# Seven half-size products for the first chunk of an MLP's second layer, in a fused attention and Fourier-mix kernel

## The chip, the cores and the metric

The kernel runs on one NeuronCore of a Trainium2 chip. A core has a matrix engine (TensorE, PE in the profile; PEld is its loading of weights), a vector engine (VectorE, DVE), a scalar engine (ScalarE, ACT), GpSimd (POOL) and a sync engine (SyncE, SP), which issues most of the transfers between the chip's main memory and the core's memory, SBUF. TensorE writes to PSUM, eight banks of 2 KB for each of 128 partitions. Every engine works through its own instructions in order and waits for others by semaphores. The metric is the time of one execution on the device in microseconds; the median of three runs before is 1942.89 us.

## The reference

Eight batches, eight heads, 576 tokens, head size 64. Attention keeps the 32 largest scores of each row; the heads are put side by side (512 channels), and then comes a Fourier mix and an MLP, all in float32:

```python
scores = scale * np.matmul(q, k.transpose(0, 1, 3, 2))
kth = np.partition(scores, -top_k, axis=-1)[..., -top_k:-top_k + 1]
scores = np.where(scores >= kth, scores, -1000000000.0)
attn = softmax(scores)                    # written out in the original
x = np.matmul(attn, v)                    # -> (8, 576, 512)
mixed = np.real(np.fft.fft(np.fft.fft(x, axis=1), axis=2))
u = x + mixed
un = (u - mean(u)) / np.sqrt(var(u) + 1e-06)
ch = np.maximum(un @ w_ch1, 0.0) @ w_ch2  # 512 -> 2048 -> 512
out = u + ch
```

## The kernel before

The attention is cut into 288 items: for each batch four pairs of heads, and for each pair nine items of 128 rows (tokens by one head, the last 32 tokens of each half of the sequence gathered into a fifth "tail" tile of 64 rows). The main loop makes one step per item. In step `i` TensorE makes the scores of item `i + 3` (`scores`, L346), transposes the exponentials of item `i - 2` (`transposes`, L411) and now and then multiplies them by v (`attend`, L448). VectorE finds the 32 largest of each row in four rounds of eight (`top_ops`, L367 and L369). GpSimd makes the two numbers of each row that the mask needs (`bounds`, `nt`) and subtracts the mask (`mask`, L384), ScalarE does the rest of the mask (L383), the exponential (`expo`, L390) and the copies out of PSUM.

When a batch's attention is done, the Fourier mix follows as matmuls with tables (`fold_ops`, `dft_tokens` L607, `dft_channels` L656), then the mean and variance (`stats`), the transposes of the mixed tile (`channels_first`, L720) and the MLP. A batch's 576 tokens are two chunks: chunk 0 has tiles 0, 1 and the tail tile 4 (320 columns), chunk 1 has tiles 2 and 3 (256 columns). `mlp_units` cuts the MLP into units: for each chunk 16 of `hidden` (first layer and relu, L742 and L746; `hT` holds the 2048 hidden channels as 16 blocks of 128), and then for each tile its part of the second layer, `back`: 16 matmuls of 512 columns into one bank `cp` (L766), in eight units of two. The tail tile has four units of L802. A tile of chunk 0 is then scaled by the inverse deviation on ScalarE (L791) and added into `x` on GpSimd (L792); tile 3 is added by VectorE (L780). `store` sends the tile out two steps later.

The order is written out by hand. Each step has a list of fixed TensorE work, and between its entries `some` takes units from the queue of the MLP. How many is set by `level`: from the units' planned costs (1.75 for a unit of `back`, 8 * width / 1200 for one of `hidden`) and the planned cost of each step's fixed work it finds the level at which the queue is empty when the next batch's MLP arrives (`arrivals`). Batch b's MLP is therefore spread over steps of the attention of batches b + 1 and b + 2. Batch 7's comes after the last attention step, alone. On GpSimd a step's order is: the mask of the item before, the plan's early work (`pool0`), `bounds`, late work (`pool`, `pool2`). SyncE issues loads of q, k and v at fixed steps, four or five steps ahead of their use, and the stores of the plan's `load2`.

The weights `w2` lie in SBUF as `w2[:, it, :]`, 16 blocks of 128 hidden channels by 512 output channels. `ps_m` is a pool of three PSUM banks, from which `hp`, `cp`, the Fourier tiles and the transposed tiles take their banks.

Of the kernel before, what the change touches and what calls it, by code (L numbers as in the profile page):

```python
# [64 lines left out]
def kernel(  # L65
# [42 lines left out]
    small = ctx.enter_context(tc.tile_pool(name="small", bufs=4))  # L108
    ps_s = ctx.enter_context(tc.tile_pool(name="ps_s", bufs=2, space=bass.MemoryType.PSUM))
    ps_t = ctx.enter_context(tc.tile_pool(name="ps_t", bufs=2, space=bass.MemoryType.PSUM))  # L110
    ps_o = ctx.enter_context(tc.tile_pool(name="ps_o", bufs=1, space=bass.MemoryType.PSUM))
    ps_m = ctx.enter_context(tc.tile_pool(name="ps_m", bufs=3, space=bass.MemoryType.PSUM))

# [36 lines left out]
    def weight_steps(chunks, space, wc, slots):  # L150
# [16 lines left out]
        def scale_high(n):  # L167
            if moe_w_ch1.dtype == F32:
                return
            scaled[n] = ps_m.tile([P, wc], F32, name=f"wh_{n}", tag="mm")  # L170
            nc.scalar.activation(
                out=scaled[n], in_=words(n)[2], func=AF.Copy, scale=2.0 ** -112
            )
# [112 lines left out]
    def scores(i, part):  # L286
# [22 lines left out]
        if part == 1:  # L309

            pool, tag = (ps_s, "sp") if i else (ps_m, "mm")
            copy = nc.scalar.copy if i else nc.vector.tensor_copy
            sp = pool.tile([P, NF * P], F32, name=f"sp_{i}_t", tag=tag)
# [164 lines left out]
    def to_tokens(pair, ch, at_once=True):  # L478
# [6 lines left out]
        pool, tag = (ps_o, "o") if at_once else (ps_m, "mm")  # L485
        tp = pool.tile([P, 4, P], F32, name=f"tpx_{pair}_{ch}", tag=tag)
# [106 lines left out]
    def dft_tokens(b, par):  # L593

# [3 lines left out]
        if b not in y_of:  # L598
            y_of[b] = batp.tile([P, 4, S], F32, name=f"y_{b}", tag="y")
        y = y_of[b]  # L600
        yps = [
            ps_m.tile([P, 2, KQ], F32, name=f"yp_{b}_{par}_{g2}", tag="mm") for g2 in range(2)
        ]

        def mm(g2, gg, st, lhsT, rows, table, start=False):

            nc.tensor.matmul(  # L607
                yps[g2][0:rows, gg, :],
# [8 lines left out]
        for g2 in range(2):  # L617
            for gg in range(2):
                g = 2 * g2 + gg
                for st in range(3):  # L620
                    f = fg[:, st] if st < 2 else ftail
                    mm(g2, gg, st, f[:, P * g:P * (g + 1)], P, gg, start=gg == 0 and st == 0)
        for st in range(3):
            mm(0, 1, st, zw[:, st, Q1:Q1 + 1] if st < 2 else ftail[:, DM:DM + 1], 1, 0)
# [5 lines left out]
        for g2, yp in enumerate(yps):  # L630
            y2 = y[:, 2 * g2:2 * g2 + 2, :]
            nc.scalar.copy(out=y2[:, :, par:HS + 1:2], in_=yp[:, :, 0:KQ - par])
            nc.scalar.copy(out=y2[:, 0, mir], in_=yp[:, 0, back])
            nc.scalar.mul(out=y2[:, 1, mir], in_=yp[:, 1, back], mul=sg[:, g2:g2 + 1])
        if par == 1:
            tails_of_y(b)
        return 4.3
# [6 lines left out]
    def dft_channels(b, t, quick=False):  # L644

        rows, y = ROWS[t], y_of[b]
        mp = ps_m.tile([P, 2, DM // 2], F32, name=f"mp_{b}_{t}", tag="mm")
# [62 lines left out]
    def channels_first(b, t):  # L710
# [7 lines left out]
        tp = ps_m.tile([P, NDT, P], F32, name=f"tpu_{b}_{t}", tag="mm")  # L718
# [5 lines left out]
        return 0.6  # L724

    def mlp_units(b):
# [4 lines left out]
        def hidden(ch, it):  # L733
# [6 lines left out]
            hp = ps_m.tile([P, CW[0]], F32, name=f"hp_{b}_{ch}_{it}", tag="mm")  # L740
# [7 lines left out]
        cps, cts = {}, []  # L748

        def ct_of(t):  # L750


            if t == 2:
                return hTs[1].rearrange("p i c -> p (i c)")[:, NIT * CW[1]:NIT * CW[1] + DM]
            if not cts:
                cts.append(batp.tile([P, 3, DM], F32, name=f"ct_{b}", tag="fold_s"))
            return cts[0][:, CHUNKS[0].index(t), :]

        def back(ch, t, part):
            n, hT, rs = CHUNKS[ch].index(t), hT_of[ch], rs_of[b]  # L760
            if part == 0:
                cps[t] = ps_m.tile([P, DM], F32, name=f"cp_{b}_{t}", tag="mm")
            cp = cps[t]
            if t != 4:
# [5 lines left out]
                if part == 7:  # L770
                    xt = x[:, t, :]

                    def store():
                        tok = HS * (t // 2) + P * (t % 2)
                        nc.sync.dma_start(out=out[b, tok:tok + P, :], in_=xt)
                        if t == 3:
                            written.add(b)

                    def finish():
                        nc.vector.scalar_tensor_tensor(  # L780
                            out=xt, in0=cp, scalar=rs[:, t:t + 1], in1=xt, op0=ALU.mult, op1=ALU.add
                        )

# [5 lines left out]
                    else:  # L789
                        ct = ct_of(t)  # L790
                        nc.scalar.mul(out=ct, in_=cp, mul=rs[:, t:t + 1])  # L791
                        nc.gpsimd.tensor_tensor(out=xt, in0=xt, in1=ct, op=ALU.add)  # L792
# [15 lines left out]
            if part == 3:  # L808
                ct = ct_of(t)
                for h in range(2):  # L810
                    r0 = TAIL + TH * h
                    nc.scalar.copy(out=ct[TH * h:TH * (h + 1), :], in_=cp[r0:r0 + TH, :])

                def finish():
                    xt, c = x[0:TAIL, 4, :], ct[0:TAIL]
                    nc.vector.tensor_tensor(out=c, in0=cp[0:TAIL], in1=c, op=ALU.add)
                    nc.vector.scalar_tensor_tensor(
                        out=xt, in0=c, scalar=rs[0:TAIL, 4:5], in1=xt, op0=ALU.mult, op1=ALU.add
                    )
                    for h in range(2):  # L820
                        tok = HS * h + 2 * P
                        nc.sync.dma_start(
                            out=out[b, tok:tok + TH, :], in_=x[TH * h:TH * (h + 1), 4, :]
                        )

                if last:
                    finish()
                else:
                    late_next.append(finish)

        units = []
        for ch in range(2):
# [4 lines left out]
            for t in CHUNKS[ch]:  # L837
# [110 lines left out]

    for b in range(B):
# [42 lines left out]
        for n, t in enumerate((0, 1, 4, 2, 3)):  # L992
# [7 lines left out]
            if first and t == 4:  # L1000
                at(s + 1, "pe", lambda: (queue.extend(held), held.clear()) and 0.0)
        at(s + 1, "begin" if quick else "dve", lambda b=b: rsqrt(b))
        arrivals.append(s + (1 if quick else 2))
        at(arrivals[-1], "units", lambda b=b: (queue if b else held).extend(mlp_units(b)))

    queue, held, pending, written, now, out_next = [], [], [], set(), [0], []
# [14 lines left out]
    def level(i):  # L1021

        steps = range(i, next((a for a in arrivals if a > i), i + PER_BATCH))
        rest, lev = sum(u[0] for u in queue + held), 0.0
# [23 lines left out]
    while i < N + 4 or plan or queue:  # L1048
# [23 lines left out]
        if pending and pending[0][0] <= i:  # L1072
# [121 lines left out]
```

## Time and profile before

| | us |
|---|---|
| median of three runs (1942.6 to 1943.57) | 1942.89 |
| the profiled execution | 1944.57 |
| its span, first to last instruction | 1942.8 |
| TensorE busy | 1831.8 |
| VectorE busy | 1577.0 |
| ScalarE busy | 1205.3 |
| GpSimd busy | 773.3 |
| L766, tiles 0 to 3 of the second layer, busy | 477.2 |
| L742, first layer, busy | 539.0 |

The profile is of one execution. A group's row names the line, the engine, the operation, what is written and read, and the size; then come the count, the busy time, the mean duration in ns of one, the idle time of the engine before it and who ended it. A float32 matmul stands there as two records, one for each pass over the moving operand. Matmuls are pipelined: a pass lasts longer than the distance to the next one. The work of the MLP lies at these times (first layer of chunk 0, then tiles 0 and 1 of the second):

| batch | first layer, chunk 0 | tiles 0 and 1 |
|---|---|---|
| 1 | 513.6 to 567.2 | 567.4 to 611.7 |
| 2 | 745.5 to 798.7 | 799.7 to 838.9 |
| 4 | 1184.9 to 1237.7 | 1238.7 to 1282.0 |
| 6 | 1624.6 to 1676.9 | 1676.7 to 1714.0 |
| 7 | 1814.2 to 1848.8 | 1848.6 to 1876.2 |

The last attention step's mask is at 1734.4 us.

### The profile page before, as it was taken

The numbers are of one execution on the slowest core, as the hardware profiler recorded it, in microseconds if no ns is written. First come the engines' busy times: TensorE is split into PE (matmuls) and PEld (weight loads), VectorE is DVE, ScalarE is ACT, GpSimd is POOL, SyncE is SP. The second block draws the span as 40 slices with busy tenths as digits, with TensorE's granted clock in tenths as the row PEclk, the third lists the DMA queues.
The fourth block names the chain that finished last, engine by engine and source line by source line (L and its number), as shares of the span: only waits on it lengthen the run. The fifth ranks groups of instructions, "written<-read, shape, count | busy, mean of one in ns | idle before, by whom it ended". The sixth has DMA issues, their size and how long they took to land.

```text
span 1942.8 us, 27224 instructions
## 1 busy us (share of the span) xinstructions
PE 1831.8 (94%) x8624; PEld 1123.4 (58%) x8624; DVE 1577.0 (81%) x3245; ACT 1205.3 (62%) x3060; POOL 773.3 (40%) x1054
## 2 busy tenths in 40 slices
PE   6567799999999999999999999999999999998999
PEld 3344465564665656556664756556664756566655
DVE  8999989999999999888888879988888879843000
ACT  6878657776876667666666667666666757541100
POOL 4768642326523454235423444235523444222000
PEclk8877899999999999999999999999999999999999
DMA  5333000101001010010100110010000100000000
GB/s 164 105 90 106 19 13 19 33 19 30 19 19 33 19 30 13 13 33 19 30 19 19 27 24 21 11 33 19 24 19 24 27 24 19 1 14 1 11 14 11
DMA packets 133583, 57.80 MB, mean 30 GB/s; under 512 B 124352, under 2 KB 124480, under 8 KB 133440
## 3 DMA queue, kind: packets, MB, share of 16 engines
q1 hardware_dynamic: 132656, 55.85, 10.8%
q8 instruction: 69, 1.13, 0.2%
q14 instruction: 74, 0.61, 0.1%
q10 hardware_dynamic: 784, 0.21, 0.0%
HBM read 46.57 MB, written 9.44 MB: 29 GB/s over the span
## 4 chain that ended last, share of the span: by engine, by line
PE 79%; DVE 7%; POOL 7%; ACT 4%; issue 3%; DMA 0%; SPq 0%; POOLq 0%; DVEq 0%; ACTq 0%
PE hp L742 24%; PE cp L766 22%; PE o L448 7%; PE tpP L411 6%; PE sp L346 6%; PE yp L607 3%; DVE m L367 3%; PE cp L802 3%; DVE wk L369 2%; PE mp L656 2%; POOL wk L384 2%; PE sp_t L316 2%; POOL w L198 1%; POOL w L197 1%; PE tpk L260 1%
## 5 line engine op out<-in xcount | busy, mean ns | idle before, releaser
L384 POOL TENSOR_TENSOR wk<-S,wk 128x576 f32<-128x576 f32 x288 | 407.2, 1414 | 907.8 <-ACT wk L383 854.6
L367 DVE MAX8 m<-wk 128x8 f32<-128x576 f32 x864 | 623.7, 750 | 5.5
L742 PE MATMUL hp<-unT,w 128*128 128x256 f32 (+1 forms) x2048 | 539.0, 410 | 3.1 <-ACT unT L723 2.1
L766 PE MATMUL cp<-w,hT 128*128 128x512 f32 x1024 | 477.2, 598 | 0.0
L742 PEld LDWEIGHTS hp<-unT,w 128*128 128x128 f32 x2048 | 373.5, 191 | 126.2 <-issue 31.4
L369 DVE MATCH_REPLACE8 wk<-m,wk 128x576 f32<-128x576 f32 x576 | 427.7, 743 | 0.0
L766 PEld LDWEIGHTS cp<-w,hT 128*128 128x128 f32 x1024 | 179.4, 190 | 180.5 <-issue 179.9
L390 ACT ACTIVATE wk<-wk,nt 128x576 f32<-128x576 f32 x288 | 225.6, 783 | 54.3 <-POOL wk L384 53.4
L411 PE MATMUL tpP<-ident,wk 128*128 128x128 f32 x1152 | 185.4, 285 | 65.6 <-ACT wk L390 42.0
L414 ACT COPY PT<-tpP 128x512 f32<-128x512 f32 (+1 forms) x320 | 171.8, 549 | 119.1 <-PE tpP L411 116.5
L383 ACT ACTIVATE wk<-S,nt 128x576 f32<-128x576 f32 x288 | 227.7, 791 | 27.9 <-POOL nt L376 26.5
L411 PEld LDWEIGHTS tpP<-ident,wk 128*128 128x128 f32 x1152 | 140.9, 145 | 162.9 <-ACT wk L390 60.9
L746 ACT ACTIVATE hT<-hp 128x320 f32<-128x320 f32 (+1 forms) x256 | 105.1, 411 | 193.3 <-PE hp L742 191.0
L367 DVE MAX8 m<-S 128x8 f32<-128x576 f32 x288 | 214.0, 743 | 12.2 <-ACT S L320 11.9
L369 DVE MATCH_REPLACE8 wk<-m,S 128x576 f32<-128x576 f32 x288 | 213.8, 742 | 0.0
L448 PE MATMUL o<-PT,v 128*64 128x256 f32 (+3 forms) x1440 | 196.0, 416 | 2.1 <-ACT PT L414 1.6
L349 ACT COPY S<-sp 128x512 f32<-128x512 f32 (+1 forms) x264 | 142.2, 590 | 65.9 <-PE sp L346 65.6
L346 PE MATMUL sp<-kT,qT 64*128 64x512 f32 (+1 forms) x528 | 162.1, 675 | 4.3 <-ACT means L934 3.3
L448 PEld LDWEIGHTS o<-PT,v 128*64 128x64 f32 x1440 | 111.7, 153 | 75.7 <-issue 17.5
L780 DVE SCALAR_TENSOR_TENSOR x<-cp,gi,x 128x512 f32<-128x512 f32 x11 | 8.2, 746 | 128.3 <-PE cp L766 128.3
L316 PEld LDWEIGHTS sp_t<-kt,qT 128*128 128x128 f32 x320 | 56.4, 197 | 53.8 <-issue 20.0
L346 PEld LDWEIGHTS sp<-kT,qT 64*128 64x128 f32 (+1 forms) x528 | 43.0, 193 | 62.8 <-issue 44.5
(126 smaller groups left out, 1822.6 us busy)
## 6 DMA issues: line engine op xcount, KB each, us to landing
space<-in_moe_w_ch_dram SPq DMA_DIRECT2D x32, 512.0 KB, 3.6
nat<-in_q_dram SPq DMA_DIRECT2D x128, 64.0 KB, 2.1
v<-in_v_dram SPq DMA_DIRECT2D x128, 64.0 KB, 2.1
out_dram<-x SPq DMA_DIRECT2D x32, 256.0 KB, 2.1
nat<-in_k_dram SPq DMA_DIRECT2D x124, 64.0 KB, 2.1
nat<-in_q_dram SPq DMA_DIRECT2D x128, 8.0 KB, 1.7
v<-in_v_dram SPq DMA_DIRECT2D x128, 8.0 KB, 1.7
nat<-in_k_dram SPq DMA_DIRECT2D x124, 8.0 KB, 1.7
```

The source lines that it names most:

```text
L346: nc.tensor.matmul(sp[r], lhsT=qT[hd, q_cols], rhs=kT[hd, :], start=True, stop=True)
L349: nc.scalar.copy(out=s_t[r, keys], in_=sp[r])
L367: ops.append(lambda src=src, m8=m8: nc.vector.max(out=m8, in_=src))
L369: ops.append(lambda src=src, m8=m8: nc.vector.match_replace(w, m8, src, NEG))
L383: nc.scalar.activation(out=w, in_=Ssb[i], func=AF.Relu, scale=-FAR, bias=Nt[i][:, 1:2])
L384: nc.gpsimd.tensor_tensor(out=w, in0=Ssb.pop(i), in1=w, op=ALU.subtract)
L390: nc.scalar.activation(out=w, in_=w, func=AF.Exp, bias=Nt.pop(i)[:, 0:1], accum_out=den_t[pair % 3][:, c:c + 1],)
L411: nc.tensor.transpose(tp[:, c, :], p_sb[:, k0 + P * c:k0 + P * (c + 1)], ident)
L414: nc.scalar.copy(out=pt[:, NF * he:NF * (he + 1), col:col + w], in_=tp[:, :, o:o + w])
L448: nc.tensor.matmul(o[D * e:D * (e + 1), c0:c1], lhsT=vv[:, c, e, :], rhs=pt[:, 2 * NF if c == NF else NF * e + c, c0:c1], start=(c == 0), ...
L742: nc.tensor.matmul(hp[:, 0:w], lhsT=w1[:, dt, P * it:P * (it + 1)], rhs=unT[:, dt, 0:w], start=(dt == 0), stop=(dt == NDT - 1),)
L766: nc.tensor.matmul(cp, lhsT=hT[:, it, P * n:P * (n + 1)], rhs=w2[:, it, :], start=(it == 0), stop=(it == NIT - 1),)
```

## The change

For batches 1 to 7, tiles 0 and 1 of the second layer are no longer two rows of 16 matmuls. Write the two tiles' hidden values as four quarters (tile by half of the 2048 hidden channels: A11, A12, A21, A22) and w2 as four quarters (half of the hidden channels by half of the output channels: B11, B12, B21, B22). The four quarters of the result are put together from seven products of quarters, each of eight matmuls of 256 columns:

| unit | product | bank, half | place of w2's part |
|---|---|---|---|
| `p2` | A12 B21 | v, low | w2_21, as it is |
| `p1` | A11 B11 | w, low | w2 |
| `p5` | (A21 + A22) T1 | v, high | w2_12 |
| `p4` | A22 T4 | w, high | w2_21 (batch 7: a place of its own) |
| `p6` | (A21 + A22 - A11) T2, onto p1 | w, low | w2_12 |
| `p3` | (A12 - that) B22, onto p5 | v, high | w2 |
| `p7` | (A11 - A21) T3, onto w low | w, low | w2_21 (batch 7: a place of its own) |

T1 = B12 - B11, T2 = B22 - T1, T3 = B22 - B12, T4 = B21 - T2. They are made once on GpSimd during batch 1's attention (`parts_of_w2`, 16 steps of two subtractions) and kept in main memory (`scr`), with copies of B12 and B21. During the products `bring` fetches them in halves of 512 KB into the places of B12 and B21 within w2, each as soon as the product before has read the half, and in the end B12 and B21 again. The sums of the hidden quarters (`mix`) are made in place in `hT` on GpSimd, in halves; they wait in a list, `sums`, which each step works off within a planned time (`some_sums`), or sooner where a product needs one (`need`). Five results are scaled on ScalarE and added into `x` on GpSimd, two are added by VectorE; in batch 7 VectorE adds all seven. Each product is two units of planned cost 1.75.

The banks of `ps_m` are given out by `bank` in turn, past those that are held; the two banks of the products are held throughout. `dft_tokens` now makes its two halves one after the other, and in batch 7 the Fourier tiles and the transposed tiles take banks of other pools. `written` is set when four tiles are stored, and `to_tokens` isn't done in the steps of an `attend` from step 76 on.

```diff
+    def bank(shape, name, hold=False):
+        while turn[0] in held:
+            turn[0] = (turn[0] + 1) % 3
+        n = turn[0]
+        turn[0] = (n + 1) % 3
+        t = ps_m.tile(shape, F32, name=name, tag=f"m{n}", bufs=1)
+        if not hold:
+            return t
+        held.add(n)
+        return t, lambda: held.discard(n)
...
+    scr = dramp.tile([P, len(OPS), NK, DH], F32, name="w2_parts", tag="w2_parts")
+    w2_12, w2_21 = w2[:, 0:NK, DH:DM], w2[:, NK:NIT, 0:DH]
+
+    def bring(o, place, part):
+        kcs = slice(NK // 2 * part, NK // 2 * (part + 1))
+        dst = place[part] if isinstance(place, list) else place[:, kcs]
+        nc.sync.dma_start(out=dst, in_=scr[:, o, kcs, :])
...
+        for out_, in0, in1 in sums[2 * half:2 * half + 2]:
+            nc.gpsimd.tensor_tensor(out=t[:, out_], in0=in0, in1=in1, op=ALU.subtract)
+        if half:
+            at(now[0] + 1, "load2", lambda: nc.sync.dma_start(out=scr[:, 0:4, kc, :], in_=t))
...
+    def some_sums(limit):
+        while sums and sums[0][1] <= limit:
+            key, us, fn, _ = sums.pop(0)
+            limit -= us
+            fn()
+            summed.add(key)
...
+            def product(name, cols, a, rhs_of, part, start):
+                dst = half_bank(name, cols)
+                for kc in range(NK // 2 * part, NK // 2 * (part + 1)):
+                    nc.tensor.matmul(
+                        dst, lhsT=h()[a][:, kc, :], rhs=rhs_of(kc), start=start and kc == 0,
+                        stop=kc == NK - 1, skip_group_check=True,
+                    )
+                return dst
...
+            def p5(part):
+                need((b, "21", part))
+                c = product("v", hi, "21", first, part, False)
+                bring(T2, w2_12, part)
+                if part:
+                    to_x(tb, hi, c, 2)
+
+            def p4(part):
+                c = product("w", hi, "22", in_second, part, False)
+                bring(T3, second, part)
+                if part:
+                    to_x(tb, lo, c, 3)
+                    mix("22", "22", "11")
+
+            def p6(part):
+                need((b, "11", part))
+                c = product("w", lo, "11", first, part, False)
+                bring(B12, w2_12, part)
+                if part:
+                    to_x(ta, hi, c, 4)
...
+            def p7(part):
+                need((b, "22", part))
+                c = product("w", lo, "22", in_second, part, False)
+                if not last:
+                    bring(B21, second, part)
+                if part:
+                    to_x(tb, slice(0, DM), c, None, lambda: (banks["w"][1](), store(tb)))
...
-            for t in CHUNKS[ch]:
+            if b and ch == 0:
+                begin, products = fast()
+                units[1:1] = begin
+                units += products
+            for t in (4,) if b and ch == 0 else CHUNKS[ch]:
...
+        planned = 1.5 * len(plan.get((i, "pool0"), [])) + 1.3 * len(plan.get((i, "pool2"), []))
         run(i, "pool0")
+        some_sums(max(2.1 - planned, 0.0))
         bounds(i)
+
+        some_sums(1.3)
```

In the program as it is built, the order on each engine is fixed. The prediction speaks of it: which instructions of other work stand on TensorE between two products, and which waits stand before a product.

## The prediction

> **What bounds the kernel now.** I read the page first: busy shares, then the slices.
>
> ```profile
> PE 1831.8 (94%) x8624; PEld 1123.4 (58%) x8624; DVE 1577.0 (81%) x3245; ACT 1205.3 (62%) x3060; POOL 773.3 (40%) x1054
> ...
> PE   6567799999999999999999999999999999998999
> ...
> DVE  8999989999999999888888879988888879843000
> ```
>
> One slice is 48.6 us. TensorE is full from the seventh slice on; before that no MLP work exists and VectorE sets the pace. A busy TensorE need not be at its peak, so I looked at the stages in which the changed products lie (batch 1 at 567 us, batch 2 at 800 us, batch 4 at 1239 us; columns: PE, PEld, DVE, ACT, POOL).
>
> ```profile
> core 0: us, PE busy (x) PEld busy (x) DVE busy (x) ACT busy (x) POOL busy (x), PEclk, DMA share, GB/s
> 567.00:612.00 45.00, 45.00 (x194) 22.68 (x192) 43.74 (x91) 29.03 (x76) 15.11 (x18) 1.00 0.11 26
> 800.00:852.00 52.00, 52.00 (x212) 23.62 (x209) 44.39 (x91) 30.09 (x77) 15.64 (x19) 1.00 0.07 18
> 1238.70:1282.00 43.30, 43.30 (x175) 20.76 (x168) 38.06 (x77) 27.38 (x69) 12.13 (x15) 1.00 0.08 21
> ```
>
> In batch 1's stage VectorE is busy for 43.74 of 45.00 us, so two engines are full. From batch 2 on VectorE has 5 to 8 us to spare, and the waits of 800 to 1640 us say for whom it waits:
>
> ```profile
> DVE wk L369 <- PE tpP_t L422: 43.9, 16, 5.0
> ```
>
> It waits for TensorE's transposes. So in batches 2 to 6 a microsecond off TensorE is a microsecond off the span, and in batch 7's MLP, where nothing else runs, all the more. The pace of one matmul pass is read there, in TensorE's timeline (start, length, count):
>
> ```profile
> 1876.40 7.09 PE L802 MATMUL cp<-w,hT 128*64 128x512 f32 x32
> 1883.42 27.89 PE L742 MATMUL hp<-unT,w 128*128 128x256 f32 x128
> 1911.15 27.63 PE L766 MATMUL cp<-w,hT 128*128 128x512 f32 x64
> ```
>
> The last pass shows its own duration, the others the distance to the next. With the groups' 0.59 us for 512 columns: (27.63 - 0.59)/63 = 0.429 us. With 0.38 us for 256 columns: (27.89 - 0.38)/127 = 0.217 us. An f32 matmul is two passes.
>
> **The products.** Removed in each of batches 1 to 7: two tiles of 16 matmuls of 512 columns, 64 passes x 0.429 = 27.5 us. Added: seven products of 8 matmuls of 256 columns, 112 passes x 0.217 = 24.3 us. TensorE gains 3.2 us a batch, 22.4 us in all.
>
> A rule speaks against this. The Trainium skill ("TensorE: Matmul & The Clock Gate", Part 3, The mechanism) lists that a weight load overlaps running matmuls only when their row groups differ. Here all use the whole array, and there are 112 loads where there were 64. With the 0.190 us that a load takes in the trace, the old batch would cost 64 x 0.619 = 39.6 us, the new one 112 x 0.407 = 45.6 us: 42 us slower over seven batches. But L742 loads new weights for each of its 128 passes of 256 columns and still starts one every 0.217 us. I take the row.
>
> **Work on other engines**, from the groups split by shape:
>
> ```profile
> L492 DVE TENSOR_TENSOR x<-tpx,rd 128x256 f32<-128x256 f32 x57 | 24.1, 423 | 55.4 <-PE tpx L488 54.0
> L414 ACT COPY PT<-tpP 128x256 f32<-128x256 f32 x64 | 21.1, 389 | 9.8 <-PE tpP L411 9.6
> L930 POOL TENSOR_TENSOR w<-w,means 128x512 f32<-128x512 f32 x16 | 20.1, 1274 | 0.0
> L792 POOL TENSOR_TENSOR x<-x,ct 128x512 f32<-128x512 f32 x14 | 17.8, 1275 | 11.3 <-ACT ct L791 9.3 <-DVE wk L369 1.9
> L549 POOL TENSOR_TENSOR zt<-x 64x256 f32<-64x256 f32 x16 | 11.3, 724 | 0.0
> L791 ACT ACTIVATE ct<-cp,gi 128x512 f32<-128x512 f32 x14 | 9.6, 688 | 8.0 <-PE cp L766 7.5
> L780 DVE SCALAR_TENSOR_TENSOR x<-cp,gi,x 128x512 f32<-128x512 f32 x11 | 8.2, 746 | 128.3 <-PE cp L766 128.3
> ```
>
> GpSimd, a batch: eight sums of hT quarters at 1.27 us and five adds into x at 0.72, less two adds at 1.275 = +11.2 us. Its cover is its own idle time, 60% of the span and some 4 us of each 6 us step. What is queued behind a sum is the next nt and mask, whose exponential TensorE transposes a step later; uncovered it would cost all 11.2 us. In the built order the sums of hT come at least 9 us of TensorE work before the product that needs them (7 in batch 7). The table of w2's sums is 32 subtractions x 0.72 = 23 us once, 1.4 us in each of 16 steps where GpSimd is under half busy: nothing. ScalarE: five scalings of 0.39 for two of 0.69, +0.6 us. VectorE: 0.42 + 0.75 = +1.2 us, from the two last adds. In batches 2 to 6 its 5 to 8 us of slack hide that. In batch 1 the slack is 1.26 us against 1.2 added, so I book no gain there. In batch 7 the adds are all VectorE's, which is idle there.
>
> **Two new waits of TensorE.** First, products six and four share a bank: four writes its high half, six then accumulates in its low half. By addresses alone six needn't wait for the reader of four. The Trainium skill ("PSUM — Partial Sum Buffer", PSUM bank collisions raise a hardware error) says that two engines must be kept apart by bank even at disjoint columns; no run here shows that error, but the built order holds the wait: six starts only after the scaling of four's result. The price: the end of the last pass, 0.38 - 0.22, a reading of 0.39 (0.42 on VectorE in batch 7) and two handoffs of some 0.05, thus 0.65 us, less what stands between: one tails' product (0.25) in batches 1, 3, 4, 5, four or five transposes (0.43, 0.54) in 2 and 6, nothing in 7. That is 4 x 0.4 + 0.2 + 0.1 + 0.7 = 2.6 us. Nothing is the lower end; an exponential (0.98 with its accumulator) just ahead on ScalarE in six batches makes 8.5. I take 3.0. Behind six on TensorE stands the next step's work, and VectorE waits for that.
>
> Second, the quarters brought through SP. Behind a waiting transfer on SP stand the q, k and v loads of the next pair, used four steps (24 us) later: hidden. One transfer is 512 KB:
>
> ```profile
> space<-in_moe_w_ch_dram SPq DMA_DIRECT2D x32, 512.0 KB, 3.6
> fd<-c_fd SPq DMA_DIRECT2D x1, 512.0 KB, 6.9
> ```
>
> I take 3.6, a median of 32, plus 0.3 from TensorE's end to the issue; fd was issued into a full queue (1 KB right behind it took 6.7 us), while the queues are a tenth busy here. Against 3.9 us stands the TensorE work between the product that frees a place and the one that reads it. For sums in w2_12 it is 7 us or more (5.2 in batch 7), for those in w2_21 over 11 (8.6). Tight is only the restored w2_21: its first half is issued after the seventh product's first half, and the tail tile reads it after 8 passes (1.7) and little else: 3.0, 2.9 and 2.8 us in batches 1, 2 and 6. In 3 to 5 an attend and two scores stand between (6.8). Stalls of 0.9 + 1.0 + 1.1 = 3.0 us. Batch 7 restores nothing there.
>
> **Sum.** 22.4 - 3.0 - 3.0, less the 1.9 left of batch 1 (3.2 - 0.4 - 0.9) that VectorE doesn't let through: 14.5 us off. Span 1942.8 - 14.5 = 1928.3; the profiled execution took 1944.57, so 1930.1; it stood 1.7 above the median of 1942.89, which becomes 1928.4.
>
> The split Fourier products and the bank rotation move no instruction of any length. Batch 7's wait for its fold stays: 3.4 us of TensorE work fill it in place of 3.8.
>
> **Rivals.**
> - Full gain: the waits vanish in TensorE's lead over the others. Batches 2 to 7 give 6 x 3.2 = 19.2, or 22.4 with batch 1: 1920.5 to 1923.7. For it: TensorE's waits from 800 to 1640 us sum to under 5 us. Against: TensorE is in order and the tail tile comes right behind.
> - Half lost: ScalarE's five extra reads or GpSimd's sums hold back masks and copies, so half of batches 2 to 6 (12.0 us after waits) goes: 6.0 + 2.5 in batch 7 = 8.5, 1934.4. Against: VectorE waits for TensorE now.
> - All of it lost but batch 7: 1940.4, no measurable change.
> - Slower: the transfers land late. At fd's 6.9 us the restored quarter stalls batches 1, 2 and 6 by 4.2 to 4.4, batches 3 to 5 by 0.4, product six in batch 7 by 2.0: 16.1 us in place of 3.0. After such idle the clock falls, as the trace shows at the fold (5.09 idle, then 1.31 us where four passes later take 0.66; granted clock 0.59 over the next 7.3 us):
>
> ```profile
> 1764.71 1.31 PE L607 MATMUL yp<-fs,fg 128*128 128x145 f32 x4 [5.09 <-DVE fg L533]
> ...
> 1780.30 0.66 PE L607 MATMUL yp<-fs,fg 128*128 128x145 f32 x4
> ```
>
> Three such stalls at 3.0 us (0.41 x 7.3) add 9.0. Then 17.5 - 16.1 - 9.0 = 7.6 us slower, 1950.5. It decides from a landing of some 6.5 us.
>
> That the change doesn't do what it says is out: the built order holds 56 products of 256 columns in each of seven batches.
>
> **Numbers.** Likeliest 0.58 (own range 1925 to 1932), full gain 0.17, half lost 0.11, all lost 0.07, late transfers 0.07. Under 0.2% (3.9 us) a measurement of this kernel can't tell from no change: faster 0.86, same 0.07, slower 0.07. The range leaves out the slower case, all lost, and the last part of the full gain: 1921.5 to 1939.
>
> **What would show it.** Products at 0.217 us a pass, batch 4's stage from hidden layer to tail tile some 3 us shorter; a wait of 0.4 us before product six, put down to ScalarE's scaling; a wait of 1 us before the tail tile in batches 1, 2 and 6, put down to a transfer of w2_parts that lands in 3.6 us; VectorE still waiting for TensorE from 800 us on. I am wrong if the transfers land later than 4.5 us, if passes are slower than 0.23 us, or if VectorE ceases to wait.

## The result, and the profile after

The changed kernel takes 1930.8 us (median of four runs, 1930.58 to 1932.15); the kernel before took 1942.78 us beside it. The ratio is 0.9939, with a 95% interval of 0.9922 to 0.9956: 12.0 us less, where 14.5 were forecast. The profiled execution took 1930.58 us, its span is 1928.8 us.

The page of the changed kernel: busy time by engine, two rows of the slices, and the transfers that bring the quarters (count, size, median us to landing).

```profile
PE 1808.0 (94%) x8960; PEld 1185.2 (61%) x8960; DVE 1584.8 (82%) x3262; ACT 1209.6 (63%) x3078; POOL 871.7 (45%) x1160
...
PE   6567799999999999999999999999999999998999
...
DVE  8999989999999989989898989998798989852110
...
w<-w_parts SPq DMA_DIRECT2D x78, 512.0 KB, 4.4
```

TensorE has 336 passes more (48 in each of seven batches) and is busy for 23.8 us less. GpSimd has 98 us more. What bounds the kernel is unchanged. A quarter's half lands in 4.4 us, not in the 3.6 that I took. Between 800 and 1640 us VectorE still waits for TensorE's transposes:

```profile
DVE wk L386 <- PE tpP_t L439: 45.8, 15, 5.0
```

The pace is plainest in batch 7, where the seven products run alone (TensorE's timeline: start, length, count):

```profile
1837.60 3.62 PE L1025 MATMUL cv<-w,hT 128*128 128x256 f32 x16
1841.05 3.62 PE L1025 MATMUL cw<-w,hT 128*128 128x256 f32 x16
1844.51 3.62 PE L1025 MATMUL cv<-w,hT 128*128 128x256 f32 x16
1847.96 3.62 PE L1025 MATMUL cw<-w_s,hT 128*128 128x256 f32 x16
1852.20 3.69 PE L1025 MATMUL cw<-w,hT 128*128 128x256 f32 x16 [0.63 <-issue]
1855.73 3.62 PE L1025 MATMUL cv<-w,hT 128*128 128x256 f32 x16
1859.18 3.62 PE L1025 MATMUL cw<-w_s,hT 128*128 128x256 f32 x16
1862.73 3.65 PE L893 MATMUL cp<-w,hT 128*64 128x512 f32 x16
```

Sixteen passes take 3.45 us from start to start. Between the fourth row and the fifth there are 4.24 us: product six waits 0.79 us for the reading of product four (the profile names no releaser here; own_bank below shows it). The rest, 25.13 - 0.79 = 24.34 us, is 112 passes at 0.217 us. From the start of batch 4's first layer to its tail tile 97.3 us became 93.7, near the 3 us that the prediction named as a sign.

The added work, in the groups split by shape:

```profile
L970 POOL TENSOR_TENSOR hT<-hT 128x512 f32<-128x512 f32 x56 | 71.3, 1274 | 53.0 <-ACT hT L831 45.5 <-PE cw L1025 7.5
L997 POOL TENSOR_TENSOR x<-x,ct 128x256 f32<-128x256 f32 x30 | 21.6, 730 | 3.0 <-ACT ct L995 3.0
...
L995 ACT ACTIVATE ct<-cw,gi 128x256 f32<-128x256 f32 x18 | 8.5, 474 | 12.1 <-PE cw L1025 11.8
...
L983 DVE SCALAR_TENSOR_TENSOR x<-cw,gi,x 128x512 f32<-128x512 f32 x7 | 5.2, 743 | 3.0 <-PE cw L1025 3.0
```

GpSimd's 1.27 and 0.73 us and VectorE's 0.74 are as forecast; ScalarE's scaling takes 0.47 us in place of 0.39, and VectorE's add of 256 columns 0.48 in place of 0.42.

A second view I worked out from the traces: the time from the first matmul of one batch's first layer to that of the next. "To 1" runs from the first busy instruction to batch 1's, "batch 7" to the end of VectorE's last add. The row of the kernel before is in us, the others are differences from it. The names are those of the experiments below.

```
                          to 1   batch 1  batch 2  3 to 5  batch 6  batch 7
before                   513.6    231.8    219.5    659.7   189.5    125.2
changed                   +0.1     +1.6     -1.4     -7.5    -4.1     -2.4
changed, again            +1.3     +1.5     -1.3     -7.5    -4.5     -2.4
from_two                  +0.7     +2.0     -1.2     -7.5    -3.0     -2.4
own_bank                  +1.0     +0.7     -1.6     -9.3    -4.9     -2.5
tail_first                -1.6     -0.6     -2.9     -9.4    -4.4     -1.3
table_only                +1.0     +2.0     +1.2     -1.6    -2.9      0.0
edits_only                -3.4     +2.0     +1.1     -1.7    -2.4      0.0
table_split               -2.1     +1.4     -1.4     -7.5    -3.5     -2.4
late_restore              +0.7     +1.4     -1.3     -5.1    -3.8     -2.4
split_tail_bank           -1.8     -0.6     -3.2    -10.3    -6.1     -2.8
```

Kernels that do the same in the first column differ there by up to 2.8 us (+1.3 to -1.6): by 275 us, ahead of all products and sums, the changed kernel's own two executions are 2.6 us apart. Little can be read from one entry of that column. From batch 1 to batch 5 such kernels agree within 0.2, and in batch 6 within 1.5.

### The profile page after: what moved, and what is told of

Read it like the earlier page. It is cut to its first block, busy times and chain, and to the rows that moved or that the text cites. A ratio compares the mean times of both kernels' runs of the same rounds, so it can differ in the third digit from the quotient of the medians.

```text
span 1928.8 us, 28145 instructions
## 1 busy us (share of the span) xinstructions
PE 1808.0 (94%) x8960; PEld 1185.2 (61%) x8960; DVE 1584.8 (82%) x3262; ACT 1209.6 (63%) x3078; POOL 871.7 (45%) x1160
## 4 chain that ended last, share of the span: by engine, by line
PE 80%; POOL 7%; ACT 5%; DVE 3%; issue 3%; DMA 1%; SPq 0%; POOLq 0%; DVEq 0%; ACTq 0%
PE hp L827 25%; PE cp L854 11%; PE o L465 8%; PE sp L363 6%; PE tpP L428 6%; PE cw L1025 4%; PE cv L1025 4%; PE yp L629 4%; PE mp L677 3%; PE cp L893 3%; POOL wk L401 2%; PE sp_t L333 2%; DVE m L384 1%; POOL w L215 1%; POOL w L214 1%
## 5 line engine op out<-in xcount | busy, mean ns | idle before, releaser
L854 PE MATMUL cp<-w,hT 128*128 128x512 f32 x576 | 268.9, 598 | 2.5 <-ACT hT L881 2.5
L854 PEld LDWEIGHTS cp<-w,hT 128*128 128x128 f32 x576 | 100.8, 190 | 104.0 <-issue 98.4
L1025 PE MATMUL cw<-w,hT 128*128 128x256 f32 x416 | 99.3, 383 | 2.4 <-issue 1.2
L970 POOL TENSOR_TENSOR hT<-hT 128x512 f32<-128x512 f32 x56 | 71.3, 1274 | 53.0 <-ACT hT L831 45.5
L1025 PEld LDWEIGHTS cw<-w,hT 128*128 128x128 f32 x416 | 75.4, 190 | 19.4 <-issue 6.1
```

Source lines behind the costliest of these rows:

```text
L854: nc.tensor.matmul(cp, lhsT=hT[:, it, P * n:P * (n + 1)], rhs=w2[:, it, :], start=(it == 0), stop=(it == NIT - 1),)
L1025: nc.tensor.matmul(dst, lhsT=h()[a][:, kc, :], rhs=rhs_of(kc), start=start and kc == 0, stop=kc == NK - 1, skip_group_check=True,)
```

## The experiments

Each was timed beside runs of the kernel before, which took 1944.1, 1944.35, 1944.12 and 1943.45 us in the four groups in which they ran. Differences "to the changed kernel" are to its second median, 1930.95.

**after_again**: the changed kernel unedited.

> The changed kernel once more, as the mark for the other three. Theory (the gain of the sum is right, the profile of before was an execution some 1.7 us longer than its median): again 12 us less than before, 1930.8 us, and span 1928.8 to 1929.1 us. Rival (14 us is the true gain and the median drew late executions): 1929 us.

1930.95 us, ratio 0.9933 [0.992, 0.9945]. The gain stands, at 12 to 13 us.

**own_bank**: product four gets a bank of its own, freed after its reading, so product six needn't wait for that reading.

```diff
             def p4(part):
-                c = product("w", hi, "22", in_second, part, False)
+                c = product("u", lo, "22", in_second, part, True)
                 bring(T3, second, part)
                 if part:
                     to_x(tb, lo, c, 3)
+                    banks["u"][1]()
```

> Product four gets a bank of its own, so product six no longer waits for the reading of four. Theory (TensorE's waits are paid in full): the trace of the changed kernel shows 0.55, 0.34, 0.55, 0.55, 0.55, 0.23 and 0.79 us ahead of product six in batches 1 to 7, 3.6 in all; all but batch 1's come off: 3.0 us less than the changed kernel, 1927.8. Rival (TensorE only waits elsewhere, for ScalarE, a little later): within 0.7 us of the changed kernel.

1927.55 us, ratio 0.9915 [0.9902, 0.9929]: 3.4 us under the changed kernel. TensorE in batch 3, the changed kernel first (the 16 passes of product six are the last row and those after it):

```profile
1038.98 1.89 PE L1025 MATMUL cw<-w,hT 128*128 128x256 f32 x8
1040.71 0.38 PE L333 MATMUL sp_t<-kt,qT 128*128 128x128 f32 x2
1041.48 1.97 PE L1025 MATMUL cw<-w,hT 128*128 128x256 f32 x8 [0.39 <-POOL nt L393]
```

and with the bank of its own:

```profile
1040.41 0.38 PE L333 MATMUL sp_t<-kt,qT 128*128 128x128 f32 x2
1040.63 1.89 PE L1025 MATMUL cw<-w,hT 128*128 128x256 f32 x8
```

From the tails' product to product six 0.77 us became 0.22. The profile puts the wait down to GpSimd's `nt`, an instruction that product six has no use for; taking product four out of the bank ended it, so it was the reading of four. By the same measure the seven waits of the changed kernel are 0.55, 0.34, 0.55, 0.55, 0.55, 0.23 and 0.79, 3.6 us together.

**tail_first**: the tail tile ahead of the products, where B21 is still in its place; T1 can then be fetched only after the tail tile.

```diff
             def begin():
                 for part in range(2):
-                    bring(T1, w2_12, part)
...
+            def first_sum():
+                for part in range(2):
+                    bring(T1, w2_12, part)
...
-                units += products
             for t in (4,) if b and ch == 0 else CHUNKS[ch]:
...
+            if b and ch == 0:
+                units += products
```

> The tail tile goes ahead of the seven products, so nothing reads the restored quarter of w2 for some 30 us. Theory: the waits of 1.3, 1.3 and 1.4 us ahead of the tail tile in batches 1, 2 and 6 go; batch 1's is worth nothing, VectorE being full there: 2.5 to 4 us less than the changed kernel, 1926.8 to 1928.3. Rival (the transfers were hidden, the wait only covers another): no change. Against both: the first sum for product five is now fetched only after the tail tile; if it lands late, a new wait appears ahead of product five and nothing is gained.

1925.82 us, ratio 0.9908 [0.9895, 0.9922]: 5.1 us under the changed kernel, and that with 1.1 us lost again in batch 7, where product five now waits for T1:

```profile
PE cv L1023 <- DMA w<-w_parts: 0.9, 1, 0.9
```

What it takes away, in the changed kernel's batch 1:

```profile
607.03 1.89 PE L1025 MATMUL cw<-w,hT 128*128 128x256 f32 x8
608.76 0.60 PE L428 MATMUL tpP<-ident,wk 128*128 128x128 f32 x4
609.19 0.27 PE L439 MATMUL tpP_t<-ident,wk 128*128 128x128 f32 x1
609.40 1.07 PE L893 MATMUL cp<-w,hT 128*64 128x512 f32 x2
611.15 1.93 PE L893 MATMUL cp<-w,hT 128*64 128x512 f32 x6 [0.68 <-DMA w<-w_parts]
```

The tail tile's first two passes start at once, the third waits for the restored quarter. The eighth pass starts 3.09 us after the first in place of the 1.34 us of an unhindered group. Counted from the last product, batches 1, 2 and 6 lose 1.75, 1.75 and 1.4 us: 4.9 us. Beyond these, batches 3 to 5 gain 2.0 us, though the tail tile had no wait there: the new order puts other work ahead of product six, whose waits of 0.55 us become 0.23, which is 1.0 of it; the other 1.0 I did not trace.

**from_two**: batch 1 keeps its two old tiles.

```diff
-            if b and not last:
+            if b > 1 and not last:
...
-            if b and ch == 0:
+            if b > 1 and ch == 0:
...
-            for t in (4,) if b and ch == 0 else CHUNKS[ch]:
+            for t in (4,) if b > 1 and ch == 0 else CHUNKS[ch]:
```

> Batch 1 keeps the old tiles 0 and 1, batches 2 to 7 have the seven products. Theory (in batch 1 VectorE is the bound, and the products cost it 1.2 us and TensorE two waits): 1.5 us less than the changed kernel, 1929.3, batch 1's stretch from first layer to first layer 231.9 us as before in place of 233.4. Rival (batch 1's saving reaches the end like any other): 1.5 to 3.2 us more, 1932.3 to 1934.0.

1932.28 us, ratio 0.9939 [0.9927, 0.9952]: 1.3 us over the changed kernel, where my theory wanted 1.5 less. In batch 1's own stage it is 0.4 us; most of the rest lies in batch 6's, which the edit doesn't touch. Nor is the comparison of batch 1 a clean one: without its products a tile of chunk 1 starts 1.79 us late there, as in edits_only below, which in the changed kernel it doesn't. That TensorE's time counts in batch 1 too is shown by own_bank (0.9 us less in batch 1's stage) and tail_first (2.2 less).

**table_split**: each step of the table stores its own two results, into one tile that lives through the sixteen steps.

```diff
-        if half == 0:
-            parts[kc] = batp.tile([P, 4, DH], F32, name=f"w2_t_{kc}", tag="fold_d")
-        t, lo, hi = parts[kc], w2[:, kc, :], w2[:, NK + kc, :]
+        if not parts:
+            parts[0] = batp.tile([P, 4, DH], F32, name="w2_t", tag="fold_d")
+        t, lo, hi = parts[0], w2[:, kc, :], w2[:, NK + kc, :]
...
-        if half:
-            at(now[0] + 1, "load2", lambda: nc.sync.dma_start(out=scr[:, 0:4, kc, :], in_=t))
+        two = slice(2 * half, 2 * half + 2)
+        at(now[0], "load2", lambda: nc.sync.dma_start(out=scr[:, two, kc, :], in_=t[:, two]))
```

> Each step of the table of w2's sums stores its own two subtractions (256 KB) at once, into one tile that lives through all sixteen steps, in place of one store of 512 KB a step after the pair into a tile that is used again. Theory (GpSimd's wait for the store of the tile before, 16.0 us in 5 waits in the first attention, makes the masks about 2 us late and nothing gives that back): those waits go, the stage of batch 0 loses about 1.5 us of the 1.6 us that it gained, and the time is 1.5 to 2 us under the changed kernel's 1930.9, at about 1929. Rival (the subtractions themselves, 23 us on GpSimd, make the masks late): no change within 0.5 us.

1927.97 us, ratio 0.9915 [0.9901, 0.9928]: 3.0 us under the changed kernel. GpSimd's waits between 330 and 400 us (us in total, times, longest), in the changed kernel:

```profile
POOL w_t L784 <- DMA w_parts<-w_t: 16.0, 5, 6.2
POOL wk L401 <- ACT wk L400: 9.0, 6, 3.4
```

and with the stores split:

```profile
POOL wk L401 <- ACT wk L400: 26.2, 12, 4.9
POOL w_t L784 <- DMA w_parts<-w_t: 3.1, 1, 3.1
```

In the changed kernel GpSimd waited for the store of the tile before it, with masks behind it in its order. With the stores split it mostly waits for ScalarE again. The loss is at this place: from 357 to 401 us VectorE's items fall 2.5 us behind those of the kernel before in table_only and in both executions of the changed kernel, and by nothing in table_split and edits_only. The theory named the right wait, but at 1.5 to 2 us too small a cost. The rival falls: the subtractions are still there.

**table_only** and **edits_only**: no products in any batch; all tiles are computed as in the kernel before. The first still makes the table (first part of the diff, and so in the two other conditions), the second leaves out its sixteen steps and two copies as well (second part).

```diff
-            if b and ch == 0:
+            if b > 99 and ch == 0:
...
-    for kc in range(NK):
-        for half in range(2):
-            at(
-                PER_BATCH + 14 + 2 * kc + half, "pool",
-                lambda kc=kc, half=half: parts_of_w2(kc, half),
-            )
-    for o, place in ((B12, w2_12), (B21, w2_21)):
-        at(PER_BATCH + 14, "load2", lambda o=o, place=place: nc.sync.dma_start(
-            out=scr[:, o], in_=place
-        ))
```

On TensorE, VectorE and ScalarE the two have the same order. What is left in both, beside the kernel before, are the banks in turn, the halves of `dft_tokens`, batch 7's Fourier and transposed tiles in banks of other pools, and the later `to_tokens` in batch 5.

> The table of w2's sums and the edits around it (banks taken in turn, half steps of the transform of tokens, the order of late stores), with no products of quarters in any batch: the kernel before plus what is done once. Theory (the table costs about 2 us in the first attention): 1 to 3 us over the kernel before, with the stage of batch 0 longer by about 1.6 us and every later stage as before. Rival (the loss in batch 0's stage is variation from run to run, and the table is hidden): the same as the kernel before within 0.7 us, and no wait of GpSimd for the store that delays a mask.

1943.95 us, ratio 0.9999 [0.9991, 1.0007]: level with the kernel before, and my theory of 1 to 3 us more fell as it stood. But the profile showed the table's loss in the first column and a gain in batches 3 to 6, so:

> The kernel of the table alone without the table too: what is left of the change is the banks taken in turn, the Fourier products' one-row passes moved ahead by one group, and a few transposes of xT that come one step later in batch 5; on TensorE, VectorE and ScalarE the order is that of the kernel with the table alone, and GpSimd and SP do what they did before. Theory (the table costs about 3.7 us in the first attention and these edits give about as much back later, which is why the table alone measured level with the kernel before): 3 to 4.5 us under the kernel before, at 1940 to 1941, with the stage of batch 0 as before and that of batch 6 shorter by about 3 us. Rival (the table is covered by work that waits anyway, and both sides are variation from run to run): level with the kernel before and with the table alone, within 1 us.

1940.65 us, ratio 0.9985 [0.9979, 0.9992]. The edits without the table gain 3.5 us (1.6 to 4.1 by the interval), and the table costs 3.3 us. The theory held for the time. Where the gain lies is shown only in part: from batch 1 on the edits gain no more than 1.0 us (the row of edits_only above), and the rest would be in the first column, where executions of one program differ by 2.8. In batches 3 to 5 TensorE's waits of 0.52, 0.26 and 0.50 us for VectorE's readings are gone. The largest gain that the traces show is at the start of batch 7, where nothing else covers the Fourier mix. TensorE before:

```profile
1780.30 0.66 PE L607 MATMUL yp<-fs,fg 128*128 128x145 f32 x4
...
1785.23 1.99 PE L656 MATMUL mp<-fd,y 128*128 128x256 f32 x8 [0.96 <-ACT y L634]
...
1796.97 0.66 PE L720 MATMUL tpu<-ident,x 128*128 128x128 f32 x4 [0.35 <-DVE x L662]
1797.47 1.88 PE L766 MATMUL cp<-w,hT 128*128 128x512 f32 x4
```

and with the edits alone:

```profile
1777.51 0.66 PE L629 MATMUL yp<-fs,fg 128*128 128x145 f32 x4
...
1781.52 1.89 PE L677 MATMUL mp<-fd,y 128*128 128x256 f32 x8
...
1792.20 1.04 PE L742 MATMUL tpu<-ident,x 128*128 128x128 f32 x8
1793.08 1.88 PE L854 MATMUL cp<-w,hT 128*128 128x512 f32 x4
```

From the second transform's first pass to the channel products 4.93 us became 4.01: ScalarE reads one half of the tokens' transform while TensorE makes the other. To the last row 17.17 became 15.57. About 0.5 us of that is the second group of transposed tiles (`tpu`), which waited for VectorE's reading of a Fourier tile and no longer does, now that these tiles have banks of other pools. The edits have a price as well: 2.0 and 1.1 us in batches 1 and 2, where a tile of chunk 1 now starts 1.79 and 0.94 us late behind ScalarE's reading of the tile before it (more on this below). In batch 1 of edits_only:

```profile
694.66 1.98 PE L854 MATMUL cp<-w,hT 128*128 128x512 f32 x4 [1.62 <-ACT hT L881]
```

**twice**: every transfer of a quarter is issued twice.

```diff
-        nc.sync.dma_start(out=dst, in_=scr[:, o, kcs, :])
+        for _ in range(2):
+            nc.sync.dma_start(out=dst, in_=scr[:, o, kcs, :])
```

> Every transfer that brings a quarter of w2 or of its sums is issued twice into the same place, so that what waits for it waits for twice the bytes: a landing of some 8.5 to 9 us in place of 4.4. Theory (the changed kernel lives within about 2 us of the point where late transfers decide; the prediction put that point at a landing of some 6.5 us): TensorE waits ahead of product six in every batch and ahead of the tail tile in batches 1, 2 and 6, together 15 to 30 us over the changed kernel's 1930.9, so slower than the kernel before or level with it. Rival (the other work that TensorE is given between the products covers the second transfer too): at most 4 us over the changed kernel, all of it ahead of the tail tile.

2084.15 us, ratio 1.0718 [1.0703, 1.0733]: 153 us over the changed kernel, far outside both expectations. It was not a doubled landing: each second transfer waits on SP for the first to land, and everything behind it on SP waits too. First SP's wait of that kind (us in total, times, longest), then TensorE in batch 4:

```profile
SPq L771 <- DMA w<-w_parts: 328.9, 78, 5.4
```

```profile
1353.91 1.07 PE L894 MATMUL cp<-w,hT 128*64 128x512 f32 x2
1367.15 3.67 PE L894 MATMUL cp<-w,hT 128*64 128x512 f32 x6 [12.16 <-DMA w<-w_parts]
```

The tail tile's eighth pass comes 14.5 to 14.9 us later than in the changed kernel in each of batches 3 to 5. After 12.16 us of idling its six passes take 3.67 us for 1.93, the granted clock is 0.70 from 1367 to 1376 us, and its mean over the span is 0.947 for 0.969.

**ahead**: ahead of every such transfer one of 256 KB goes into a place that nothing reads.

```diff
+        k0 = kcs.start
+        nc.sync.dma_start(out=idle[:, o, part, :, 0:DH], in_=scr[:, o, k0:k0 + 2, :])
         nc.sync.dma_start(out=dst, in_=scr[:, o, kcs, :])
```

> Ahead of every transfer that brings a quarter of w2 or of its sums, a transfer of 256 KB in pieces of 1 KB goes into a place that nothing reads, on the same queue and with no wait between the two: a later landing, some 6 to 6.6 us in place of 4.4, without the second transfer's wait for the first that the twofold transfers had. Theory (the prediction's point: late transfers decide from a landing of some 6.5 us): waits of 3 to 4 us ahead of the tail tile in batches 1, 2 and 6, small ones elsewhere, and a lower clock after them: 6 to 14 us over the changed kernel's 1930.9. Rival (TensorE's other work covers the longer landing, and the twofold transfers cost what they did because each waited for the one before on SP): at most 3 us over it.

1931.48 us, ratio 0.9939 [0.9926, 0.9951], 0.5 us over the changed kernel. The quarters did land later, in 5.3 us for 4.4 in the median, and TensorE's other work covered that. But it settles nothing on late landings ahead of the tail tile: the added transfers wait for no product, so SP issued many of them microseconds early (ahead of the restored quarter of batch 1, 5.7 us early), and the tail tile was met 0.1 to 0.2 us later in batches 1 and 2.

**late_restore**: both halves of B21 are issued after the whole of product seven.

```diff
-                if not last:
-                    bring(B21, second, part)
+                if part and not last:
+                    bring(B21, second, 0)
+                    bring(B21, second, 1)
```

> The two transfers that restore w2's lower left quarter are both issued after the whole of product seven, in place of one after each half: the first half of the quarter, which the tail tile reads first, is issued some 2.2 us later (in batch 1 of the changed kernel the first half of product seven ends about there ahead of the second), with nothing else on any queue moved. It asks what a microsecond of lateness ahead of the tail tile is worth, as the twofold transfers and the transfers with one ahead of them did not tell it. Theory (TensorE sets the pace there, so lateness counts whole): the wait ahead of the tail tile grows by some 2.2 us in batches 1, 2 and 6 and by at most 0.3 us in 3 to 5, so 6 to 8 us over the changed kernel's 1930.9, at 1937 to 1939; if the clock falls after a wait of some 3.5 us as the prediction's slower rival said, up to 9 us more. Rival (TensorE gives the wait back in its lead over VectorE): at most 3 us over it.

1933.13 us, ratio 0.9948 [0.9934, 0.9961]: 2.2 us over the changed kernel, which by the numbers is the rival's. But the edit did not act where I had put it. In batches 1, 2 and 6 nothing stands between the two halves on SP, which issues the first as soon as it may, wherever it is written. It acts in 3 to 5, where the loads of v now stand ahead of the first half. SP in batch 4, changed kernel:

```profile
1270.62 0.38 SPq L770 DMA_DIRECT2D w<-w_parts  x1
1271.04 2.04 SPq L231 DMA_DIRECT2D v<-in_v_dram  x4
1273.13 1.93 SPq L247 DMA_DIRECT2D v<-in_v_dram  x4
1275.16 0.38 SPq L770 DMA_DIRECT2D w<-w_parts  x1
```

and in this one:

```profile
1269.64 2.88 SPq L231 DMA_DIRECT2D v<-in_v_dram  x4
1272.57 1.85 SPq L247 DMA_DIRECT2D v<-in_v_dram  x4
1274.52 0.93 SPq L770 DMA_DIRECT2D w<-w_parts  x2
```

The tail tile's eighth pass then starts 6.36, 7.16 and 6.87 us after the last product in batches 3 to 5, where it had been 5.99 in each: 2.4 us of waits, and batches 3 to 5 are 2.4 us longer. A wait ahead of the tail tile counts whole. No fall of the clock came with these waits of up to 1.2 us (granted 1.00 in the 10 us around each); longer ones were not tried by themselves.

**split_tail_bank**: the three remedies together, the tail tile first in batches 1 to 6 only.

> Three changes to the changed kernel together: the table's stores split as above, the tail tile ahead of the products in batches 1 to 6 alone (batch 7 keeps its order), and product four in a bank of its own. Theory (the three losses are in three places and add up: about 2 us, 5.1 + 1.2 us, 3.4 us): about 10 us under the changed kernel's 1930.9, at 1920 to 1922. Rival (the waits that are taken away come back as VectorE's or GpSimd's lateness, as these engines are the next to end): less than 7 us under it, at 1924 or more, with more waits of TensorE for transposes and masks in the attention steps.

1919.41 us, ratio 0.9869 [0.9855, 0.9882]: 11.5 us under the changed kernel and 25 under the kernel before, the fastest of all. Its theory held. The sum of the three, 3.0 + 5.1 + 1.1 + 3.4 = 12.6, is not quite reached, since tail_first had already shortened some of product six's waits.

**split_tail_bank_relief**: the same, and in batch 1 the two last adds go from VectorE to ScalarE and GpSimd.

```diff
-                if n is None or last:
+                eased = n is None and not last and b == 1
+                if (n is None and not eased) or last:
...
-                r = room(n)
+                if eased:
+                    n = 5 if e == 1 else 6
+                r = room(0 if n == 6 else n)
```

> The kernel of the three changes together, and in batch 1 alone the two last adds of the products leave VectorE: ScalarE scales the two halves out of PSUM (0.39 us each) and GpSimd adds them into x (three adds of 0.72 us). Theory (in batch 1 it is TensorE that sets the pace, as that batch's saving did arrive in the changed kernel): within 0.7 us of the three changes together, 1919.4. Rival (the prediction's: batch 1's VectorE is full, so 1.2 us off it is 1.2 us off the span): 1 to 2 us under it, the difference in batch 1's stage.

1919.59 us, ratio 0.9878 [0.9865, 0.9892], and batch 1's stage is as long as without it (-0.6): VectorE's 1.2 us cost nothing over the stage. At 690 us VectorE is 0.4 us ahead of where it is without the edit, and by 707 us that is gone, in a wait of TensorE that the next section shows.

## Why the prediction was right, and where it was not

The time lies in the likeliest case's range, and its main terms hold. But two of them were too small, and three things that I had booked at no effect, or at no gain, have one. These largely cancel, so that the number came so close is in part luck.

- **Products, 22.4 us gained**: holds. The pace is 0.217 us with new weights for each pass, so the weight-load rule that I weighed against the row does not hold here; it would have put the change at 42 us slower.
- **Product six behind the reading of four, 3.0 us**: 3.6 by the trace, 3.4 by own_bank. My sum came to 2.6, each wait 0.1 to 0.15 us too small; the scaling (0.47 us, not 0.39) is 0.08 of that, and the rest I did not trace. I expected it under ScalarE's name; the profile gave it another in batch 3.
- **The restored quarter, 3.0 us**: the places (batches 1, 2, 6) are right. The size is 4.9 us, as the landing is 4.4 us and not 3.6, just under the 4.5 that I had named as a sign of being wrong: 0.8 more in three places gives 5.4. My nearest row was 512 KB too, from main memory into other places; it is still a median of 3.5 in the changed kernel.
- **"So I book no gain there" for batch 1, 1.9 us**: no gain came, but not for the reason that I gave. VectorE is 97% busy in that window, but own_bank and tail_first show batch 1's stage following TensorE, and relief shows that VectorE's adds are covered. Still the stage is 1.6 us longer than before. Counted from the stage's start, the changed kernel is 0.4 us ahead up to 702 us, and then it loses 2.2 us, most of it in a wait that the kernel before doesn't have. On GpSimd the add of a chunk 1 tile now stands ahead of a step's fold and `nt`, where it stood behind them, and waits for ScalarE's scaling. So the mask behind it and its exponential are late, and TensorE's transposes come 2.61 us after the scores ahead of them, where it was 1.06:

```profile
696.10 1.27 POOL L883 TENSOR_TENSOR x<-x,hT 128x512 f32<-128x512 f32 x1 [3.02 <-ACT hT L881]
703.09 0.66 PE L428 MATMUL tpP<-ident,wk 128*128 128x128 f32 x4 [0.95 <-ACT wk L407]
```

  That is read from the trace; no run took this wait away, and it is still in the fastest kernel.
- **The table of w2's sums, "nothing"**: failed, 3.3 us. I priced its 23 us of subtractions against GpSimd's idle time and did not ask what the subtraction itself waits for: the store of the tile before, issued a step later on a queue that waits for TensorE. Half-busy was no cover, because a wait in an in-order engine holds the masks behind it.
- **"The split Fourier products and the bank rotation move no instruction of any length"**: failed, by edits_only 3.5 us of gain. In batch 7's start there is no cover, so ScalarE's earlier reading is worth 0.9 us and the other banks of the transposed tiles about 0.5. Not all of the 3.5 could be placed. The rotation also costs: in the changed kernel's batches 3 to 5 tile 3 of chunk 1 waits for ScalarE's reading of tile 2, which the kernel before doesn't do (batch 4, TensorE):

```profile
1354.62 1.88 PE L854 MATMUL cp<-w,hT 128*128 128x512 f32 x4
1357.28 1.98 PE L854 MATMUL cp<-w,hT 128*128 128x512 f32 x4 [0.78 <-ACT hT L881]
```

  The start is 0.94 us late, three times: 2.8 us. That a bank just freed is the next in turn is my reading; no run took this wait away, and it is still in the fastest kernel.

The sum again: 22.4 - 3.4 - 4.9 - 2.8 - 3.3 + 3.5 = 11.5 us. The 3.5 were measured without products and hold batch 2's wait of 0.94 us, which the changed kernel doesn't have; batch 1's 1.79 us are replaced by the wait above and one of 0.25 ahead of the tile, 1.8 together. That makes 12.4 us, against 12 to 13 measured. In batches 3 to 5, where a stage repeats, it closes nearly: a batch gains 3.2 - 0.55 - 0.94 = 1.7 us over the edits, and (7.5 - 1.7) / 3 = 1.9 is measured. In the other batches it closes within some 0.5 us.

Of the rivals, full gain did not come, because the waits do not vanish in a lead: late_restore has them one for one. Half lost would have needed ScalarE or GpSimd to hold back batches 2 to 6; there the waits of TensorE named above account for the stages, within those 0.5 us. Only in batch 1 did GpSimd hold a mask back. The slower case needs a later landing than there is. Its threshold of 6.5 us stays untested, since neither twice nor ahead delayed the landing alone.

## What to carry to other kernels

An added step on a half-idle engine is free only if its own operands are free: list what each added or moved instruction waits for (a tile's last store above all) and what stands behind it in that engine's order. Where one engine sets the pace, its added waits count whole, and the cheapest cure is order and room: read a place before it is overwritten, give a result its own bank. Edits that move no work still move who waits for whom, so price them at the places that have no cover.

## What had not been expected of the hardware

- A transfer of 512 KB from main memory lands in 4.4 us here (3.8 to 6.0) and in 3.5 us in another place of the same kernel; which difference between the two does it was not tried.
- ScalarE's scaled copy of 256 columns out of PSUM takes 0.47 us here, against 0.39 for a plain copy of the same size in the kernel before.
- After 12.16 us without work TensorE's next six passes took 3.67 us in place of 1.93 (in the run **twice**).
